# A linear-attention and feed-forward kernel: one small transposition goes from the tensor engine to a transposing transfer, and one denominator from matmuls to VectorE

## The chip, the core and the metric

The kernel runs on one core of a Trainium2 chip. The metric is the device time of one execution in microseconds (us); smaller is better. Before the change the median of three runs is 283.37 us (283.28 to 283.57).

## What is computed

Linear attention with phi(x) = elu(x) + 1 for 8 batches, 8 heads, 576 tokens and 64 channels a head, and then a feed-forward layer over all 4608 tokens. Inputs and output are float32; the kernel works in bfloat16 with float32 sums.

```
def phi(x):
    return np.where(x > 0, x, np.exp(x) - 1.0) + 1.0
q_p, k_p = (phi(q), phi(k))
kv = np.einsum('bhsd,bhse->bhde', k_p, v)
z = np.sum(k_p, axis=2)
num = np.einsum('bhsd,bhde->bhse', q_p, kv)
den = np.einsum('bhsd,bhd->bhs', q_p, z)[..., None] + 1e-06
attn = num / den
# x: attn as (4608 tokens, 512)
h = x @ w_in            # 512 -> 2048
g = h - np.tanh(h)
out = g @ w_out         # 2048 -> 512
```

## The kernel before, in words

**Chunks and slots.** The feed-forward layer runs in nine chunks of 512 tokens (loop over `c`). Chunks 0 to 7 hold the first 512 tokens of a batch each, chunk 8 the last 64 tokens of all eight batches (the "rest"). A chunk has two stages. Stage 1 has 16 slots `s1[0..15]`: in each, four matmuls of 128x512 (L458) make one block of `h`; after every second slot ScalarE takes the tanh of two blocks (L464) and VectorE subtracts, which writes `gT` (L465). Blocks go through PSUM banks 0 to 5 in turn, so block 6 needs bank 0 back, which the first subtraction of the chunk frees. Stage 2 has 16 slots `s2[0..15]` of four matmuls each (L479); four slots make one tile of 128 tokens, which ScalarE copies out (L490) and SyncE (SP) stores in two transfers (L503).

**Attention in the gaps.** The attention of a later batch is put into the slots by hand as lambdas. Each engine works in the order in which its instructions are written down; a scheduler changes nothing. In chunk `c`, with `n1 = c + 1` and `n2 = c + 2`, the batch `n2` gets its phi (`a_kphi`, `a_qphi`: exp on ScalarE L151, two operations on VectorE L152 and L153), its `kv` matmuls (L198, together with a column that sums `k`, which is `z`) inside `a_num`, and batch `n1` its numerator matmuls (`num_mm` L279, `rest_mm` L288).

**Two ways to divide.** Batches 0 to 2 (`b < QS`) make the denominator with matmuls (`a_den`, L371) and multiply the numerator by the reciprocal; for batch 2 the reciprocal goes out to DRAM and comes back spread over partitions (`a_spread`: `ds` L400, `rdb` L403, both on SP), and `num_scale` (L429) writes `xT`. Batches 3 to 7 divide q before the numerator: `kz_copy` copies `z` out of PSUM repeated 64 times (`zr`, L218); `q_zb` turns `zr` by two matmuls against an identity (L227) and ScalarE copies the result to `zb` (L230); GpSimd (POOL) multiplies phi(q) by `zb` in two halves (`q_prod`, L237); VectorE sums over the channels in four pieces (`q_den`, L242); `q_scale` takes the reciprocal (L248), GpSimd scales phi(q) (L251), and a transposing transfer issued by SP (`a_qT_dma`, L170) turns it for the numerator matmuls.

**Where these stand.** `a_num` is in `s2[12]` for `c == 1` and in `s2[9]` after that; `q_zb` and `q_prod` two slots later. For `c > 1` the first two `q_den` are in `s2[15]`, which puts them on VectorE ahead of the next chunk's first `gT`. The float32 loads of `k`, `q` and `v` are issued by GpSimd (L104): those of batch `n2 + 1` in `s2[9]` for `c` from 2 to 4, those of batch 3 in `s1[0]` and those of batch 4 in `s2[15]` of chunk 1. `k` and `q` have one buffer each, so a load waits for the last reader of the batch before.

**The rest tokens of batches 0 and 1.** `r_phi` (phi and a transposing transfer of `qTr`, L327) is in `s2[1]` of chunk 4; in `s2[9]` of chunk 6 `r_den` makes their denominator with eight matmuls (L335), takes the reciprocal (L338, L340) and spreads it through DRAM (L343, L347), `r_num` makes the numerators, and in `s1[3]` of chunk 7 `r_scale` multiplies (L359).

**Batch 2's k.** Its two exp are in `s1[1]` and `s1[3]` of chunk 1, its two `r` operations (L152) stand at the end of chunk 0, and its two minima (L153) in `s1[3]` and `s1[5]`. `a_den` and `a_spread` of batch 2 are in `s1[12]`.

Of the kernel before, what the change touches and what calls it, by code (L numbers as in the profile page):

```python
# [11 lines left out]
F32 = mybir.dt.float32  # L12
BF16 = mybir.dt.bfloat16
AF = mybir.ActivationFunctionType
ALU = mybir.AluOpType
# [3 lines left out]
def kernel(  # L19
# [9 lines left out]
    nc = tc.nc  # L29
    B, H, S, D = q.shape  # L30
# [58 lines left out]
    def rest_at(b):  # L89

        return 512 * B + 64 * b
# [120 lines left out]
    def kz_copy(b, b0, o):  # L212
        ps = ps_all[:, b0:b0 + 2, o:o + 132].rearrange("p g (i e) -> p g i e", i=2)
        if b < QS:
            nc.vector.tensor_mul(kz_t[b][:, :, :, 64:96], ps[:, :, :, 64:65].to_broadcast([128, 2, 2, 32]), mask)
        else:
            zr_t[b] = rpool.tile([128, 2, 2, 64], BF16, name="zr")
            nc.vector.tensor_copy(zr_t[b].rearrange("p i g t -> p g i t"),  # L218
                                  ps[:, :, :, 64:65].to_broadcast([128, 2, 2, 64]))
        nc.vector.tensor_copy(kz_t[b][:, :, :, 0:64], ps[:, :, :, 0:64])  # L220


    def q_zb(b, bank):

        ps = ps_all[:, bank, 0:256]
        for i in range(2):
            nc.tensor.matmul(ps[:, 128 * i:128 * i + 128], zr_t[b][:, i].rearrange("p g t -> p (g t)"), ident,  # L227
                             start=True, stop=True)
        zb_t[b] = rpool.tile([128, 2, 128], BF16, name="zb")
        nc.scalar.copy(zb_t[b].rearrange("p i x -> p (i x)"), ps)  # L230

    def q_prod(b):

# [48 lines left out]
    def rest_mm(b, b0, o, qT=None):  # L282

        kz, j = kz_t[b], J - 1 if qT is None else 0
        qT = qT_t[b] if qT is None else qT
        for i in range(2):
            for rs, cs, h, hg in quads():
                nc.tensor.matmul(ps_all[cs, b0 + h, 64 * i + o:64 * i + o + 64], kz[rs, hg, i, 0:64],  # L288
                                 qT[rs, i, j, hg, :], start=True, stop=True)
        return [ps_all[:, b0 + h, o:o + 128].rearrange("p (i t) -> p i t", i=2) for h in range(2)]  # L290
# [27 lines left out]
    def r_phi():  # L318

        x = qr.rearrange("p b i h d -> p (b i h d)")  # L320
        e, r = (epool.tile([128, 2, J, D], BF16, name=n).rearrange("p h j d -> p (h j d)")[:, 0:8 * D] for n in "er")
        y = const.tile([128, 8 * D], BF16, name="qpr")
        nc.scalar.activation(e, x, AF.Exp)
        nc.vector.tensor_scalar(r, x, 0.0, 1.0, ALU.max, ALU.add)
        nc.vector.tensor_tensor(y, e, r, ALU.min)
        qT_t["r"] = const.tile([128, 2, 2, 2, 64], BF16, name="qTr")
        nc.sync.dma_start_transpose(out=qT_t["r"].rearrange("p b i g t -> p (b i) (g t)"), in_=y)  # L327

    def r_den(bank, o):

        qT = qT_t["r"]
        ps = ps_all[0:64, bank, o:o + 64]
        for n, p in enumerate((0, 2, 1, 3)):
            for b in range(2):
                nc.tensor.matmul(ps[32 * b:32 * b + 32], kz_t[b][:, p // 2, p % 2, 64:96], qT[:, b, p % 2, p // 2, :],  # L335
                                 start=(n == 0), stop=(n == NP - 1))
        den = const.tile([64, 64], F32, name="denr")
        nc.vector.tensor_scalar(den, ps, 1e-6, None, ALU.add)  # L338
        rden = const.tile([64, 64], F32, name="rdenr")
        nc.vector.reciprocal(rden, den)  # L340
        ds = dram.tile([2, H, 64], F32, name="dsr")
        for b in range(2):
            nc.sync.dma_start(out=ds[b], in_=rden[32 * b:32 * b + H])  # L343
        rdb = rdb_t["r"] = const.tile([128, 2, NP, 64], F32, name="rdbr")
        for b in range(2):
            for hh in range(2):
                nc.sync.dma_start(  # L347
                    out=rdb[64 * hh:64 * hh + 64, b].rearrange("p a t -> p (a t)"),
                    in_=ds[b, 4 * hh:4 * hh + 4].rearrange("a t -> (a t)").partition_broadcast(64))

    def r_num(b0, o):

        pr_t["r"] = [rest_mm(b, b0, o + 128 * b, qT_t["r"][:, b].unsqueeze(2)) for b in range(2)]

    def r_scale():

        for b in range(2):
            for h, ps in enumerate(pr_t["r"][b]):
                nc.vector.tensor_mul(xT[:, 2 * h:2 * h + 2, rest_at(b):rest_at(b) + 64], ps,  # L359
                                     rdb_t["r"][:, b, 2 * h:2 * h + 2])  # L360

    def a_den(b, bank, parts=range(4)):

# [266 lines left out]
    for c in range(NC):  # L630
# [4 lines left out]
        if c == 0:  # L635
            sub = {}

            def spread1():
                a_spread_pe(1, range(NP))
                for p in range(NP):  # L640
                    a_scale(1, p, sub["ns"], p)

            def kv1():
                kv_cols_mm(1, 4, 0)
                kz_copy(1, 4, 0)

            def num1():
                ns = sub["ns"] = new_ns(1)
                for i in (1, 0):
                    b0 = 4 + 2 * i  # L650
                    num_mm(1, i, lambda h: b0 + h)
                    nc.scalar.copy(ns[:, i::2, 0:8, :].rearrange("p a j t -> p a (j t)"), ps_all[:, b0:b0 + 2, :])

            def vp1():
                a_vp1(0, nc.vector.tensor_copy)
                a_vp1(1, nc.scalar.copy)

            s1[13].append(lambda: a_qphi(1, 0))
            s1[14].append(lambda: a_qphi(1, 1))
            s2[0].append(lambda: a_kphi(1, 0))  # L660
            s2[2].append(lambda: ([f() for i in range(2) for f in a_qT_pe(1, i, Banks([4 + 2 * i, 5 + 2 * i]))], load_q(2)))
            s2[3].append(lambda: (a_kphi(1, 1), load_k(2)))
            s2[4].append(prepare)
            s2[6].append(lambda: a_vp(1, 0))
            s2[8].append(lambda: (vp1(), load_v(2)))
            s2[9].append(kv1)
            s2[10].append(lambda: (a_den(1, 4), num1(), a_split(1)))
            s2[13].append(spread1)

            qs, ks = [], []  # L670

            def exp2(pieces, src, store, name, i):
                pieces.append(phi_pieces(2, src, store, name, i))
                pieces[i][0]()

            def rest2(f):
                f[1]()
                f[2]()

            def k2(i):  # L680
                ks.append(phi_pieces(2, k_t, kp_t, "kp", i))
                ks[i][1]()

            s2[14].append(lambda: exp2(qs, q_t, qp_t, "qp", 0))
            s2[15].append(lambda: (exp2(qs, q_t, qp_t, "qp", 1), rest2(qs[0]), rest2(qs[1]), a_qT_dma(2), [f() for f in later], k2(0), k2(1)))
        elif n1 < B:
            if c == 1:
                def kv2():
                    kv_cols_mm(2, 6, 0)
                    kz_copy(2, 6, 0)  # L690

                s1[10].append(kv2)
            if n1 < QS:
                s1[12].append(lambda: (a_den(n1, 6), a_spread(n1)))
            else:
                if c == 2:
                    s1[2].append(lambda: (q_den(n1, 0, 0), q_den(n1, 0, 1)))
                e = 2 * (c == 2)
                s1[3 + e].append(lambda: q_den(n1, 1, 0))
                s1[5 + e].append(lambda: q_den(n1, 1, 1))  # L700
                s1[7 + e].append(lambda: q_scale(n1))
            m = 12 if c == 1 else 9
            if c == 3:
                s1[12].append(load_qr)
            if c == 4:
                s2[1].append(r_phi)
            if c == B - 2:
                s2[m].append(lambda: (r_den(7, 384), r_num(6, 128)))
            s2[m].append(lambda: a_num(n1, n2 if n2 < B else 0))
            if n2 < B:  # L710
                s2[m + 2].append(lambda: (q_zb(n2, 4 if c == 1 else 7), q_prod(n2)))
                if c > 1:
                    s2[15].append(lambda: (q_den(n2, 0, 0), q_den(n2, 0, 1)))
        if c == B - 1:
            s1[3].append(r_scale)
        if c == 1:
            for i in range(2):
                s1[1 + 2 * i].append(lambda i=i: ks[i][0]())
                s1[3 + 2 * i].append(lambda i=i: ks[i][2]())
            s1[0].append(lambda: (a_vp(2, 0, nc.gpsimd), a_vp(2, 1, nc.gpsimd),  # L720
                                  gate(qT_t[n1]), load_k(n2), load_q(n2), load_v(n2)))
        if c >= 1 and n2 < B:
# [100 lines left out]
```

## Time and profile before

| what | value |
|---|---|
| median of 3 runs | 283.37 us |
| time of the profiled execution | 283.29 us |
| span of its instructions | 281.5 us (1.79 us of the time lie outside) |
| granted TensorE clock | 1.00 |
| TensorE (PE) busy | 276.1 us (98%) |
| VectorE (DVE) busy | 176.9 us (63%) |
| ScalarE (ACT) busy | 146.0 us (52%) |
| GpSimd (POOL) busy | 81.9 us (29%) |

Busy time is the union of an engine's instructions. The profile also gives groups of instructions (count, busy time, mean duration), the idle time of an engine and what ended it, the chain of work that ended last, timelines of one engine, and for transfers the time from issue to landing (the last update of the semaphore). Queue q0 carries the loads issued by GpSimd, queue q1 the transfers issued by SP.

### The profile page before, as it was taken

How to read it: one execution, taken by the hardware profiler on the slowest of the kernel's cores; microseconds unless marked ns; L12 is line 12 of the kernel's file. 1: busy time of each engine (PE TensorE's matmuls, PEld its weight loads, DVE VectorE, ACT ScalarE, POOL GpSimd, SP SyncE). 2: the span in 40 equal slices, each digit the busy share in tenths (PEclk: the TensorE clock that was granted, in tenths of full speed). 3: DMA queues.
4: the chain of work that ended last, by engine and by line, in shares of the span. 5: the costliest groups of instructions: out<-in, count | busy, mean ns of one | idle time of the engine just before them, and what ended most of it. 6: DMA issues, size and time to landing. Idle time of an engine off the chain costs nothing.

```text
span 281.5 us, 5103 instructions
## 1 busy us (share of the span) xinstructions
PE 276.1 (98%) x2085; PEld 131.0 (47%) x2085; DVE 176.9 (63%) x285; ACT 146.0 (52%) x177; POOL 81.9 (29%) x79
## 2 busy tenths in 40 slices
PE   8899999999999999999999999999999999999995
PEld 3574544444544454445444544454444444444443
DVE  5759967993879755976398839763961177006600
ACT  4747918856255654675357636673541365126411
POOL 8642330320092434362623361406050000000000
PEclk9999999999999999999999999999999999999999
DMA  6999999799829899079904990342025210230023
GB/s 102 189 205 207 205 207 206 158 196 213 228 46 204 117 199 214 1 123 161 207 18 96 173 222 18 73 90 67 8 43 118 77 36 2 51 78 20 2 66 83
DMA packets 40135, 33.25 MB, mean 118 GB/s; under 512 B 17744, under 2 KB 35824, under 8 KB 39984
## 3 DMA queue, kind: packets, MB, share of 16 engines
q0 software_dynamic: 18688, 18.35, 41.5%
q1 hardware_dynamic: 21424, 14.58, 21.9%
q8 instruction: 16, 0.26, 0.3%
q14 instruction: 7, 0.06, 0.0%
HBM read 38.14 MB, written 9.46 MB: 169 GB/s over the span
## 4 chain that ended last, share of the span: by engine, by line
PE 91%; DMA 4%; DVE 1%; ACT 1%; issue 1%; POOL 1%; SPq 0%; DVEq 0%; POOLq 0%
PE ps_all L458 43%; PE ps_all L479 41%; DMA out_dram<-osb 3%; DMA kraw<-in_k_dram 2%; PE ps_all L198 2%; PE ps_all L742 1%; PE ps_all L279 1%; ACT osb L490 1%; SPq L503 0%; PE ps_all L309 0%; POOL qraw L101 0%; ACT e L151 0%; PE ps_all L182 0%; PE ps_all L371 0%; DVE rden L380 0%
## 5 line engine op out<-in xcount | busy, mean ns | idle before, releaser
L479 PE MATMUL ps_all<-w_out_sb,gT 128*128 128x512 bf16 x560 | 124.6, 379 | 0.0
L458 PE MATMUL ps_all<-xT,w_in_sb 128*128 128x512 bf16 x560 | 122.8, 379 | 0.0
L465 DVE TENSOR_TENSOR gT<-ps_all,th 128x1024 bf16<-128x1024 f32 x64 | 77.7, 1217 | 45.2 <-ACT th L464 45.2
L464 ACT ACTIVATE th<-ps_all 128x1024 f32<-128x1024 f32 x64 | 65.6, 1024 | 46.7 <-PE ps_all L458 46.7
L458 PEld LDWEIGHTS <-w_in_sb 128*128 128x128 bf16 x560 | 54.6, 98 | 65.7 <-issue 0.3
L479 PEld LDWEIGHTS <-gT 128*128 128x128 bf16 x560 | 53.8, 98 | 63.2 <-issue 0.2
L490 ACT COPY osb<-ps_all 128x512 f32<-128x512 f32 (+1 forms) x36 | 20.7, 582 | 56.9 <-PE ps_all L479 46.3
L237 POOL TENSOR_TENSOR pr<-qp,zb 128x1152 f32<-128x1152 bf16 x10 | 23.4, 2359 | 37.8 <-ACT zb L230 37.8
L251 POOL TENSOR_TENSOR qp<-qp,rd 128x1152 bf16<-128x1152 bf16 x10 | 21.0, 2115 | 36.9 <-issue 23.7
L242 DVE TENSOR_REDUCE dn<-pr 128x9 f32<-128x576 f32 x20 | 14.5, 746 | 12.2 <-POOL pr L237 12.2
L151 ACT ACTIVATE e<-qraw 128x1152 bf16<-128x1152 bf16 (+1 forms) x16 | 18.2, 1135 | 3.6 <-DMA qraw<-in_q_dram 3.6
L151 ACT ACTIVATE e<-kraw 128x1152 bf16<-128x1152 bf16 x15 | 17.5, 1165 | 0.0
L153 DVE TENSOR_TENSOR kp<-e,r 128x1152 bf16<-128x1152 bf16 x15 | 11.9, 792 | 4.1 <-ACT e L151 3.2
L153 DVE TENSOR_TENSOR qp<-e,r 128x1152 bf16<-128x1152 bf16 (+1 forms) x16 | 11.9, 742 | 4.0 <-ACT e L151 3.0
L568 PE MATMUL ps_all<-zero 128*128 128x512 bf16 x29 | 9.2, 475 | 1.2 <-DVE zero L513 1.2
L124 POOL DMA_DIRECT2D w_out_sb<-in_moe_w_out_dram x10 | 6.4, 637 | 10.1 <-DMA w_in_sb<-in_moe_w_in_dram 4.7
L104 POOL DMA_DIRECT2D kraw<-in_k_dram x7 | 5.5, 783 | 11.0 <-ACT e L151 10.6
L202 DVE COPY vp<-v 128x1152 bf16<-128x1152 bf16 x11 | 6.0, 542 | 4.0 <-DMA v<-in_v_dram 4.0
L470 DVE TENSOR_TENSOR gT<-ps_all,th 128x512 bf16<-128x512 f32 x12 | 7.9, 686 | 0.6
L104 POOL DMA_DIRECT2D qraw<-in_q_dram x7 | 5.3, 752 | 9.9 <-ACT e L151 5.2
L469 ACT ACTIVATE th<-ps_all 128x512 f32<-128x512 f32 x12 | 7.2, 596 | 1.9 <-DVE gT L748 1.0
L420 ACT CAST xT<-ps_all 128x1024 bf16<-128x1024 f32 x5 | 5.1, 1012 | 5.1 <-PE ps_all L288 4.4
(108 smaller groups left out, 146.8 us busy)
## 6 DMA issues: line engine op xcount, KB each, us to landing
out_dram<-osb SPq DMA_DIRECT2D x65, 128.0 KB, 2.4
kraw<-in_k_dram POOLq DMA_DIRECT2D x7, 576.0 KB, 7.0
qraw<-in_q_dram POOLq DMA_DIRECT2D x6, 576.0 KB, 8.7
v<-in_v_dram POOLq DMA_DIRECT2D x6, 576.0 KB, 12.4
w_in_sb<-in_moe_w_in_dram POOLq DMA_DIRECT2D x3, 512.0 KB, 9.8
v<-in_v_dram POOLq DMA_DIRECT2D x4, 288.0 KB, 8.7
rdb<-ds SPq DMA_DIRECT2D x2, 576.0 KB, 5.7
w_out_sb<-in_moe_w_out_dram POOLq DMA_DIRECT2D x4, 256.0 KB, 11.7
```

What stands on the lines that cost most here:

```text
L104: nc.gpsimd.dma_start(out=t[:, :, :, 0:n].rearrange("q h i j d -> q (h i) (j d)"), in_=x.rearrange("(n q) x -> q n x", n=4))
L151: return (lambda: nc.scalar.activation(e, x, AF.Exp), lambda: nc.vector.tensor_scalar(r, x, 0.0, 1.0, ALU.max, ALU.add), lambda: nc.vector ...
L153: lambda: nc.vector.tensor_tensor(y, e, r, ALU.min))
L237: nc.gpsimd.tensor_mul(pr_t[b][:, i].rearrange("p j h d -> p j (h d)"), qp_t[b][:, i].rearrange("p j h d -> p j (h d)"), zb_t[b][:, i].uns ...
L242: nc.vector.tensor_reduce(dn_t[b][:, i, :, h], pr_t[b][:, i, :, h, :], mybir.AxisListType.X, ALU.add)
L251: nc.gpsimd.tensor_mul(x, x, rd[:, i].unsqueeze(2).to_broadcast([128, J * 2, D]))
L458: nc.tensor.matmul(h, w_in_sb[:, p, fi * 128:(fi + 1) * 128], xT[:, p, c * 512:(c + 1) * 512], start=(n == 0), stop=(n == NP - 1))
L464: nc.scalar.activation(th, h, AF.Tanh)
L465: nc.vector.tensor_sub(gT[:, fi:fi + 2, :], h, th)
L479: nc.tensor.matmul(o, gT[:, fi, i * 128:(i + 1) * 128], w_out_sb[:, fi, :], start=(fi == 0), stop=(fi == NF - 1))
L490: nc.scalar.copy(osb[:, f0:f1], o[:, f0:f1])
L568: nc.tensor.matmul(ps_all[:, 0, :], zero[:, 0:128], zero, start=True, stop=True)
```

## The change

Three edits. First, `q_zb` is gone: for batches 3 to 7 `kz_copy` lets SP issue a transposing transfer `zb <- zr` (two blocks of 128x128) directly after the copy that makes `zr`. Second, the rest tokens of batches 0 and 1 are divided before their numerator: `r_z` (VectorE, `s2[13]` of chunk 3) takes their `z` from `kz`, repeats it, and a transposing transfer of four blocks makes `zbr`; `r_scale` (VectorE, `s2[12]` of chunk 4) multiplies, sums, takes the reciprocal and scales, and only then `qTr` is transposed; `r_den`, its DRAM trip and the multiplications of chunk 7 are gone, and `r_copy` copies the numerators out. Third, in chunk 1 the second `r` operation of batch 2's k moves from the end of chunk 0 to `s1[5]`, and `a_den` with `a_spread` of batch 2 from `s1[12]` to `s1[13]`. In the order of each engine nothing else moves, except that SP now has `zb` ahead of the stores of the fourth tile in chunk 1 and of the third tile in chunks 2 to 5, and `zbr` and `qTr` between stores of chunks 3 and 4.

```diff
@@ kz_copy
             zr_t[b] = rpool.tile([128, 2, 2, 64], BF16, name="zr")
             nc.vector.tensor_copy(zr_t[b].rearrange("p i g t -> p g i t"),
                                   ps[:, :, :, 64:65].to_broadcast([128, 2, 2, 64]))
+            zb_t[b] = rpool.tile([128, 2, 128], BF16, name="zb")
+            nc.sync.dma_start_transpose(out=zb_t[b], in_=zr_t[b].rearrange("p i g t -> p (i g t)"))
         nc.vector.tensor_copy(kz_t[b][:, :, :, 0:64], ps[:, :, :, 0:64])
-    def q_zb(b, bank):
-        ps = ps_all[:, bank, 0:256]
-        for i in range(2):
-            nc.tensor.matmul(ps[:, 128 * i:128 * i + 128], zr_t[b][:, i].rearrange("p g t -> p (g t)"), ident,
-                             start=True, stop=True)
-        zb_t[b] = rpool.tile([128, 2, 128], BF16, name="zb")
-        nc.scalar.copy(zb_t[b].rearrange("p i x -> p (i x)"), ps)
@@ r_phi, r_z, r_scale, r_num, r_copy
         nc.vector.tensor_tensor(y, e, r, ALU.min)
+        qp_t["r"] = y
+    def r_z():
+        zs = const.tile([128, 2, 2, 2], BF16, name="zsr")
+        zr = const.tile([128, 2, 2, 2, 64], BF16, name="zrr")
+        for b in range(2):
+            nc.vector.tensor_reduce(zs[:, b], kz_t[b][:, :, :, 64:72], mybir.AxisListType.X, ALU.max)
+            nc.vector.tensor_copy(zr[:, b].rearrange("p i g t -> p g i t"),
+                                  zs[:, b].unsqueeze(3).to_broadcast([128, 2, 2, 64]))
+        zb_t["r"] = const.tile([128, 4, 128], BF16, name="zbr")
+        nc.sync.dma_start_transpose(out=zb_t["r"], in_=zr.rearrange("p b i g t -> p (b i g t)"))
+    def r_scale():
+        y = qp_t["r"]
+        pr = const.tile([128, 8, D], F32, name="prr")
+        nc.vector.tensor_mul(pr.rearrange("p n d -> p (n d)"), y, zb_t["r"].rearrange("p n x -> p (n x)"))
+        dn = const.tile([128, 8], F32, name="dnr")
+        nc.vector.tensor_reduce(dn, pr, mybir.AxisListType.X, ALU.add)
+        nc.vector.tensor_scalar(dn, dn, 1e-6, None, ALU.add)
+        rd = const.tile([128, 8], F32, name="rdr")
+        nc.vector.reciprocal(rd, dn)
+        x = y.rearrange("p (n d) -> p n d", d=D)
+        nc.vector.tensor_mul(x, x, rd.unsqueeze(2).to_broadcast([128, 8, D]))
         qT_t["r"] = const.tile([128, 2, 2, 2, 64], BF16, name="qTr")
         nc.sync.dma_start_transpose(out=qT_t["r"].rearrange("p b i g t -> p (b i) (g t)"), in_=y)
-    def r_den(bank, o):
...
+    def r_copy(b0, o):
+        for h, copy in enumerate((nc.vector.tensor_copy, nc.scalar.copy)):
+            copy(xT[:, 2 * h:2 * h + 2, rest_at(0):rest_at(2)].rearrange("p i (b t) -> p b i t", b=2),
+                 ps_all[:, b0 + h, o:o + 256].rearrange("p (b i t) -> p b i t", b=2, i=2))
@@ the slots
             def k2(i):
                 ks.append(phi_pieces(2, k_t, kp_t, "kp", i))
-                ks[i][1]()
+                if not i:
+                    ks[i][1]()
...
-                s1[12].append(lambda: (a_den(n1, 6), a_spread(n1)))
+                s1[13].append(lambda: (a_den(n1, 6), a_spread(n1)))
...
             if c == 3:
                 s1[12].append(load_qr)
+                s2[13].append(r_z)
             if c == 4:
                 s2[1].append(r_phi)
-            if c == B - 2:
-                s2[m].append(lambda: (r_den(7, 384), r_num(6, 128)))
-            s2[m].append(lambda: a_num(n1, n2 if n2 < B else 0))
+                s2[12].append(r_scale)
+            s2[m].append(lambda: (c == B - 2 and r_num(6, 128), a_num(n1, n2 if n2 < B else 0),
+                                  c == B - 2 and r_copy(6, 128)))
             if n2 < B:
-                s2[m + 2].append(lambda: (q_zb(n2, 4 if c == 1 else 7), q_prod(n2)))
+                s2[m + 2].append(lambda: q_prod(n2))
...
-        if c == B - 1:
-            s1[3].append(r_scale)
...
-                s1[3 + 2 * i].append(lambda i=i: ks[i][2]())
+                s1[3 + 2 * i].append(lambda i=i: (i and ks[i][1](), ks[i][2]()))
```

More of the change, by code (lines that the diff above doesn't have):

```diff
@@ L326, in r_phi @@
         qT_t["r"] = const.tile([128, 2, 2, 2, 64], BF16, name="qTr")
         nc.sync.dma_start_transpose(out=qT_t["r"].rearrange("p b i g t -> p (b i) (g t)"), in_=y)
-    def r_den(bank, o):
[L331 to L341, printed above, removed]
-        for b in range(2):
[L343 to L360, printed above, removed]
+    def r_num(b0, o):
+        for b in range(2):
+            rest_mm(b, b0, o + 128 * b, qT_t["r"][:, b].unsqueeze(2))
```

## The prediction

> **What bounds the kernel now.** I read the page first: who is busy, and which engine makes the chain.
>
> ```profile
> PE 276.1 (98%) x2085; PEld 131.0 (47%) x2085; DVE 176.9 (63%) x285; ACT 146.0 (52%) x177; POOL 81.9 (29%) x79
> PE 91%; DMA 4%; DVE 1%; ACT 1%; issue 1%; POOL 1%; SPq 0%; DVEq 0%; POOLq 0%
> ```
>
> PE is busy for 98% of the span at a granted clock of 1.00, and its matmuls run back to back (64 of 128x512 in 13.81 us, 0.2158 us each). So every matmul taken off PE is time off the end, and every wait put before one is added to it. Next the chain of waits, at the places that the change touches: the start of chunk 1, one stage 2, and the numerators of chunk 6.
>
> ```profile
> 47.29 9.64 PE ps_all L458 x44
> ...
> 103.34 0.11 PE ps_all L227 x2
> 103.45 3.45 PE ps_all L479 x16
> 106.90 13.81 PE ps_all L458 x64
> ...
> 216.75 0.24 PE ps_all L335 x8
> 216.99 0.02 issue
> 217.01 0.23 DVE denr L338
> 217.24 0.04 issue
> 217.28 0.32 PE ps_all L288 x15
> 217.60 0.43 PE ps_all L279 x8
> ```
>
> The two turning matmuls cost 0.11 us a batch, the eight denominator matmuls with what follows 0.85 us, and the 44 matmuls of chunk 1 take 0.14 us more than 44 x 0.2158 = 9.50. Third, since `zb` has its readers on GpSimd and VectorE, their timeline around one of these places (chunk 2 into 3):
>
> ```profile
> 101.57 0.42 DVE L218 CAST zr<-ps_all 128x256 bf16<-128x256 f32 x1 [0.58 <-PE ps_all L198]
> 104.32 4.68 POOL L237 TENSOR_TENSOR pr<-qp,zb 128x1152 f32<-128x1152 bf16 x2 [2.34 <-ACT zb L230]
> 106.71 1.42 DVE L242 TENSOR_REDUCE dn<-pr 128x9 f32<-128x576 f32 x2 [3.05 <-POOL pr L237]
> 109.72 1.23 DVE L465 TENSOR_TENSOR gT<-ps_all,th 128x1024 bf16<-128x1024 f32 x1 [1.60 <-ACT th L464]
> ```
>
> VectorE waits 3.05 us for the first half of `pr`, and the chunk's first `gT` is queued behind that. Last, how long SP's transfers take there: the view of the stores from 97 to 109 us, its columns least, median and most, then the queues from 162.3 to 165.9 us.
>
> ```profile
> DMA to landing us min/median/max: 5.7/6.0/6.3
> q0 software_dynamic: 601, 0.67, 117.1%
> ```
>
> Queue q1 has no line in the second answer: in these 3.6 us it moved not one packet, though a store issued at 162.30 was waiting. The same holds from 105.5 to 107.4 and from 134.3 to 136.9. In chunk 5, where nothing is loaded, the stores take 2.2/2.3/2.4.
>
> **Part by part.** *What PE loses.* Five `q_zb`: 5 x 0.11 = 0.55. In chunk 6 the stretch from 216.75 to the numerators at 217.60 (0.85) shrinks to the sixteen L288 matmuls, 2 x 0.06 by the rows of eight in other chunks, plus 0.13 for the first small matmul after the large ones (L279 takes 0.56 there and 0.43 here): 0.25. Saved 0.60. Together 1.15 us. PE has nothing to fill in, so all of it counts.
>
> *Batch 2's k.* VectorE runs both `r` from 50.44 to 51.26, and the first `gT` of chunk 1 starts at 51.18, though its tanh was done at 50.24; it ends at 52.40, and block 6 starts at 52.45 where 47.12 + 24 x 0.2158 = 52.30 was due. That is the 0.14. With one `r` (0.41) less the `gT` ends near 52.0 and the wait goes. The moved `r` (0.45) makes the `kz` copy of batch 2 later (about 59.8 for 59.3), and `a_den`, one slot (0.86) later, just clears it. Late next is the last `gT` of the chunk: add and reciprocal (0.30 + 1.05) now stand ahead of it, so it ends near 65.0, against a first use near 65.2. I take 0.14 saved, with 0 to 0.14 as bounds.
>
> *Batch 2's reciprocal.* It is ready near 63.8 for 62.2. Its way is `ds`, then `rdb` on SP, then L429. In before `rdb` lands at 75.84 and L429 starts at 75.94; its fourth piece is ready 2.48 later at 78.42, and PE wants it at 77.63 + 5 x 0.216 = 78.71. Of this cover of 0.29, PE's own 0.25 lead (0.14 + 0.11) eats nearly all, so a later `rdb` is a stall of the same length. How much later? The `ds` transfers took 4.1 us from issue to landing, where the same kind (`dsr`) took 1.2 in chunk 6: they lay behind stores that landed until 65.57. If the stores set it, `rdb` moves by 0; if the 4.1 repeats, by 1.6. In the same stretch the load of batch 3's k waits for the moved `r`: 56.3 for 55.9. I take 0.3, nearer to the stores.
>
> *The way of z.* Before: `zr` ends at 101.99, the matmuls, a copy on ScalarE (0.38), and `zb` is there at 104.24. After: SP issues the transfer at 102.04 (it is free: the stores before it were issued by 100.28). No row shows a transfer of two transposed blocks. `qTr` (four blocks) landed 2.44 after issue with nothing loading, `qT` (eighteen) 4.65; the line through them gives 2.1 for two. In between loads the nearest rows are the stores, 128 KB to 64.
>
> How late may it be? `pr` starts 0.08 after `zb` and its half takes 2.36; two L242 and the `gT` behind them take 2.54, and with two hand-overs (0.08) `gT` ends 5.06 after `zb`. Block 6 of chunk 3 is due at 106.74 + 5.18 = 111.92, and 0.11 earlier without L227: `zb` must land by 106.75, which is 4.7 after its issue. The same sum gives 4.7 for chunks 3 and 4 (issues at 131.25 and 160.35).
>
> Chunk 1 (4.7 does not apply, the sums are in slots 2 and 5 and have 2 us to spare) and chunk 5 (no loads, 2.1) cost nothing. In chunks 2, 3 and 4 GpSimd's loads run: stores took 6.0, 5.5 and 6.1 (the medians; least 5.7, 4.7 and 6.1, most 6.3, 6.5 and 6.1). Less 0.2 for the smaller transfer (2.1 against 2.3) and less 4.7, PE stalls 1.1 + 0.6 + 1.2 = 2.9. The bounds: with the least, 0.8 + 0 + 1.2 = 2.0; with the most, 1.4 + 1.6 + 1.2 = 4.2; and with 2.1, none at all. I take 2.9, since every store that was issued while a load ran took at least 3.9, and `zb`, issued 0.7 to 1.5 us after the load of q, is inside.
>
> [...]
>
> *The rest tokens.* `r_z` on VectorE: two reductions (0.16, L617) and two copies (0.23 to 0.43): 0.8 to 1.2, in chunk 3 after the `xT` copies, inside the 3.05 in which VectorE waits for `pr`. `r_scale` in chunk 4: two products of 512 (0.43 by L325 to 0.68 by L429), a sum of 512 (0.74 by L242), 0.17 and 0.38: 2.2 to 2.7, in the same 3.05, which a late `zb` only widens. If it overran by all of 2.7, the first `gT` would take 1.6 of it in idle time and PE 0.9, so at most 0.2 would show. Their two transfers stand on SP ahead of stores, whose buffers are five tiles (17 us) deep; `qTr` is needed 50 us later. `r_copy` adds 0.38 to ScalarE before a copy that waited 0.68 for PE, and 0.43 to VectorE in a 6.76 gap. Nothing for all of these; ScalarE's five copies of 0.38 go, also for nothing.
>
> **Sum** against the profiled execution of 283.29: - 1.15 - 0.14 + 0.3 + 2.9 = + 1.9, 285.2; the median stood 0.08 above it, so 285.3.
>
> **Rivals.** *Faster: the transfer is in time.* If `zb` lands within 4.7 us of its issue in all three chunks (its packets slip through at the seam between the loads of k and q, as q1's did from 131.0 to 132.5, 226 packets of it), PE keeps the 1.29: 282.1, or 282.4 with the 0.3 of `rdb`. For it: the queue had finished its stores just before each of the three spots. Against it: the medians above. It decides at 4.7. *Worse: it misses the seam everywhere* and lands with the store issued after it (110.04, 140.11 and 168.09): 3.3, 4.2 and 3.0 later than allowed at the very most, 10.5 in sum; with the store's own time from issue in its place (6.05, 6.91, 5.78) it is 1.35 + 2.2 + 1.1 = 4.65, and with `rdb` late by 1.3 the total is 283.37 - 1.29 + 4.65 + 1.3 = 288.0. *No change:* one chunk alone stalls (1.2), with 0.1 for `rdb`: 283.4. That the change does not do what it says can be left out: PE's order has the ten and the eight matmuls gone.
>
> **How the numbers follow.** Some stall in two or three chunks, 0.68 (forecast 285.3; of this 0.1 above 288.0); one chunk alone, 0.07; in time everywhere, 0.25. A difference of 0.2% (0.57 us) is about what a measurement of this kernel can tell from none, so these are the chances of slower, same and faster. The range holds the faster case whole and the late one to 288.0: 282.1 to 288.0, with about 0.1 above it and a little below. The slower case alone would run from 284.1 (stalls of 2.0, no `rdb`) to 288.0.
>
> **What would show it.** Right: `zb` lands 5 to 6.5 after its issue in chunks 2 to 4 and 2.1 in chunk 5; VectorE waits 5 and not 3.05 us for `pr`; PE has waits on `gT` at block 6 of chunks 3, 4 and 5, of about 1 us each, and none in chunk 6. L227 and L335 are gone, and the 44 matmuls of chunk 1 take 9.50. Wrong: `zb` lands within 4.7, or VectorE puts its first `gT` elsewhere; then PE has no new wait and the time is near 282.

## The result and the profile after

| | before | after |
|---|---|---|
| median, us (lowest to highest) | 283.54 (283.28 to 284.01) | 296.29 (293.88 to 298.11) |
| profiled execution, us (its span) | 283.29 (281.5) | 295.85 (294.1) |
| PE busy, us | 276.1 | 278.8 |

The changed kernel is slower: the ratio is 1.0437, with a 95% interval from 1.0383 to 1.0491. The prediction said slower, but 285.3 us with a range to 288.0, so the size was far off. Line numbers below are those of each kernel; in the changed one L227, L335 and their followers are gone, stage 1's matmuls are L453, `gT` L460, `pr` L229, the sums L234 and the numerators' scaling L424.

The page after, two lines: who is busy, and the granted clock in 40 slices.

```profile
PE 278.8 (95%) x2067; PEld 130.8 (44%) x2067; DVE 178.6 (61%) x289; ACT 144.8 (49%) x173; POOL 82.0 (28%) x79
PEclk9999999999999999899999998899999999999999
```

PE has 18 matmuls fewer and is busy 2.7 us longer, and three slices have an 8: twice PE ran at a lower clock. The prediction's sum has no term for that. Next, what PE waited for (us in total, times, longest):

```profile
PE ps_all L453 <- DVE gT L460: 7.8, 3, 3.1
PE ps_all L453 <- DVE xT L424: 1.4, 3, 1.1
```

The first line is the predicted wait, three times over, at 2.6 us each in place of 1; the second is the late `rdb` of batch 2. The timelines around the start of chunk 3 (start, duration, what, idle time before and its releaser), from 103 us of GpSimd and of VectorE, and from 112 of PE:

```profile
111.32 4.68 POOL L229 TENSOR_TENSOR pr<-qp,zb 128x1152 f32<-128x1152 bf16 x2 [7.38 <-DMA zb<-zr]
```

```profile
113.71 1.41 DVE L234 TENSOR_REDUCE dn<-pr 128x9 f32<-128x576 f32 x2 [8.10 <-POOL pr L229]
115.04 2.35 DVE L460 TENSOR_TENSOR gT<-ps_all,th 128x1024 bf16<-128x1024 f32 x2
```

```profile
111.83 2.10 PE L453 MATMUL ps_all<-xT,w_in_sb 128*128 128x512 bf16 x9
116.31 5.95 PE L453 MATMUL ps_all<-xT,w_in_sb 128*128 128x512 bf16 x19 [2.38 <-DVE gT L460]
```

GpSimd waits for `zb`, VectorE for `pr` (8.10 us, where it was 3.05), the first `gT` stands behind the sums, and PE stands behind that `gT`. The nineteen matmuls from there on take 5.95 us where 18 x 0.2158 + 0.38 = 4.26 was due: seven of them are spaced 0.43 us. Last, the transfers of `zb` from issue to landing in us (least, median, most). The view has only the two whose semaphore updates are all recorded, those of chunks 3 and 4; by the last update of each, chunks 2, 3 and 4 are 7.26, 7.21 and 7.94, and chunk 5, without loads, is 2.72:

```profile
DMA to landing us min/median/max: 7.2/7.6/7.9
```

**The account.** Stalls, as the end of the waiting matmul less that of the one before and less 0.216: 2.54 + 2.49 + 3.31 = 8.34 for `gT`, 1.93 for `rdb`. Two stretches of half clock: 1.7 + 1.6. Saved: 1.15 + 0.14. That makes + 12.3, and the profiled execution is 12.6 longer; the other 0.3 lies in the start-up, since chunk 1 begins at 47.41 and in the kernel before at 47.12. The six times differ by how many such stretches they have, by the mean clock: 293.88 and 294.16 at 0.994, 295.85 to 296.99 at 0.988, 298.11 at 0.983, some 1.7 us for each.

### The profile page after: what moved, and what is told of

Same layout as the page of the kernel before. It is cut to its first block, busy times and chain, and to the rows that moved or that the text cites. A ratio compares the mean times of both kernels' runs of the same rounds, so it can differ in the third digit from the quotient of the medians.

```text
span 294.1 us, 5065 instructions
## 1 busy us (share of the span) xinstructions
PE 278.8 (95%) x2067; PEld 130.8 (44%) x2067; DVE 178.6 (61%) x289; ACT 144.8 (49%) x173; POOL 82.0 (28%) x79
## 5 line engine op out<-in xcount | busy, mean ns | idle before, releaser
L453 PE MATMUL ps_all<-xT,w_in_sb 128*128 128x512 bf16 x560 | 126.9, 386 | 9.2 <-DVE gT L460 7.8
L460 DVE TENSOR_TENSOR gT<-ps_all,th 128x1024 bf16<-128x1024 f32 x64 | 77.5, 1218 | 40.3 <-ACT th L459 40.1
L453 PEld LDWEIGHTS <-w_in_sb 128*128 128x128 bf16 x560 | 55.4, 99 | 78.3 <-issue 15.5
L229 POOL TENSOR_TENSOR pr<-qp,zb 128x1152 f32<-128x1152 bf16 x10 | 23.4, 2358 | 56.7 <-DMA zb<-zr 56.7
L234 DVE TENSOR_REDUCE dn<-pr 128x9 f32<-128x576 f32 x20 | 14.5, 746 | 25.2 <-POOL pr L229 25.2
L415 DVE CAST xT<-ps_all 128x1024 bf16<-128x1024 f32 x5 | 6.1, 1217 | 7.0 <-PE ps_all L280 7.0
L563 PE MATMUL ps_all<-zero 128*128 128x512 bf16 x29 | 8.5, 445 | 1.2 <-DVE zero L508 1.2
## 6 DMA issues: line engine op xcount, KB each, us to landing
w_in_sb<-in_moe_w_in_dram POOLq DMA_DIRECT2D x3, 512.0 KB, 10.5
v<-in_v_dram POOLq DMA_DIRECT2D x4, 288.0 KB, 8.9
```

What stands on the lines that cost most here:

```text
L229: nc.gpsimd.tensor_mul(pr_t[b][:, i].rearrange("p j h d -> p j (h d)"), qp_t[b][:, i].rearrange("p j h d -> p j (h d)"), zb_t[b][:, i].uns ...
L234: nc.vector.tensor_reduce(dn_t[b][:, i, :, h], pr_t[b][:, i, :, h, :], mybir.AxisListType.X, ALU.add)
L453: nc.tensor.matmul(h, w_in_sb[:, p, fi * 128:(fi + 1) * 128], xT[:, p, c * 512:(c + 1) * 512], start=(n == 0), stop=(n == NP - 1))
L460: nc.vector.tensor_sub(gT[:, fi:fi + 2, :], h, th)
L563: nc.tensor.matmul(ps_all[:, 0, :], zero[:, 0:128], zero, start=True, stop=True)
```

## The experiments

Of each run the time stands beside that of the kernel before on the same chip (283.7 to 283.8).

**One edit at a time: `z_only`.** The kernel before with the first edit alone.

```
...
+            nc.sync.dma_start_transpose(out=zb_t[b], in_=zr_t[b].rearrange("p i g t -> p (i g t)"))
...
-                s2[m + 2].append(lambda: (q_zb(n2, 4 if c == 1 else 7), q_prod(n2)))
+                s2[m + 2].append(lambda: q_prod(n2))
```

> Only the first edit on the kernel before: zb by the transposing transfer, nothing else. Theory A (the late zb makes the loss): PE loses 5 x 0.11 = 0.55 us of matmuls, zb lands 7 to 8 us after its issue in chunks 2, 3 and 4, and block 6 of the next chunk waits for what goes beyond 4.7 us: 2.5 + 2.5 + 3.3 = 8.3 us, with one to three stretches of half clock behind these waits at 1.7 us each. Time 293 to 296.5 us. Theory B (VectorE's rest-token work and SP's two extra transfers, or batch 2's late rdb, make the loss): without them little is left, at most the 2.9 us of the prediction, 282.8 to 285.7 us. Where the granted clock shows no stretch below full, the time under theory A is 291.

Measured 293.29 us (291.44 to 294.49), ratio 1.0318 (1.0281 to 1.0355). PE's waits in its profile:

```profile
PE ps_all L460 <- DVE gT L467: 7.3, 3, 3.0
```

Theory A holds. This execution took 292.67: 283.72 - 0.55 + stalls of 2.20 + 3.14 + 2.45 + one stretch of half clock at 1.7 = 292.7. The fastest run, 291.44, has a mean clock of 0.999 and so no such stretch; the stalls alone make 283.72 - 0.55 + 7.8 = 291.0.

**`rest_only`.** The kernel before with the second edit alone (`r_z`, `r_scale`, `r_copy` for `r_den` and its DRAM trip, as in the diff above).

> Only the second edit on the kernel before: the rest tokens' denominators on VectorE. Theory A: PE loses 0.60 us at the numerators of chunk 6, and nothing is late: 282.8 us. Theory B (the VectorE work of chunks 3 and 4 pushes the first gT of the next chunk, or zbr and qTr on SP push stores): 0.2 to 3 us of waits of PE on gT at the starts of chunks 4 and 5: 283.5 to 286 us.

Measured 283.71 us, ratio 0.9993 (0.9978 to 1.0008): no difference, where theory A wanted 0.9 us. The 0.60 is there: from the numerators of chunk 5 to the stage-2 matmul behind those of chunk 6 PE takes 29.83 us, before 30.43. But the profile has two new stalls, 0.29 at the start of chunk 2 (`rdb`, whose `ds` took 4.0 to 4.8 us in this execution) and 0.15 at block 6 of chunk 5, so 0.16 is left of it. The second one comes from VectorE and GpSimd, whose timelines around it are:

```profile
164.47 1.70 DVE L345 TENSOR_SCALAR dnr<-dnr 128x8 f32<-128x8 f32 x1
166.21 0.20 DVE L347 RECIPROCAL rdr<-dnr 128x8 f32<-128x8 f32 x1
166.44 2.58 DVE L349 TENSOR_TENSOR qpr<-qpr,rdr 128x512 bf16<-128x512 bf16 x1
```

```profile
163.78 4.70 POOL L236 TENSOR_TENSOR pr<-qp,zb 128x1152 f32<-128x1152 bf16 x2 [2.34 <-DVE prr L342]
```

An addition to eight numbers takes 1.70 us and ends at 166.17, when GpSimd's first product (2.35 of the 4.70, from 163.78) has just ended at 166.13; the multiplication then lasts until 169.02, past the end of the second at 168.48. In the changed kernel, where `pr` starts later, the same two take 0.17 and 0.69. VectorE's sum just before (L344, from 163.75 to 164.44) ran beside the same GpSimd product and kept its 0.69. The reciprocal between the two ran beside the second product and took 0.20, in the changed kernel 0.20 as well. So the addition and the multiplication are long beside a GpSimd product and the sum and the reciprocal are not; why these two, no run shows.

**`k2_only`.** The kernel before with the third edit alone.

```
-                ks[i][1]()
+                if not i:
+                    ks[i][1]()
...
-                s1[12].append(lambda: (a_den(n1, 6), a_spread(n1)))
+                s1[13].append(lambda: (a_den(n1, 6), a_spread(n1)))
...
-                s1[3 + 2 * i].append(lambda i=i: ks[i][2]())
+                s1[3 + 2 * i].append(lambda i=i: (i and ks[i][1](), ks[i][2]()))
```

> Only the third edit on the kernel before: the second r operation of batch 2's k in slot 5 of chunk 1, a_den and a_spread one slot later. Theory A (the account of the changed kernel): the wait of 0.14 us at block 6 of chunk 1 goes, rdb lands about 2 us later than the 75.84 of before, and PE loses what exceeds the cover of 0.29, less 0.14 + 0.11 that is no longer there to be eaten: 1.6 us at the start of chunk 2. Time 284.9 us. Theory B (the prediction: rdb hardly later): 283.3 us.

Measured 285.50 us, ratio 1.0051 (1.0033 to 1.0069). Its waits of PE:

```profile
PE ps_all L458 <- DVE xT L429: 0.8, 3, 0.4
PE ps_all L279 <- DMA qT<-qp: 0.7, 1, 0.7
```

The size is nearer to theory A's 284.9, the make-up only in part. `rdb` lands at 77.58 for 75.84 (0.40 of this is a later start-up) and costs 0.53 + 0.38 + 0.33 = 1.24 us of stalls (the view counts less, since it leaves the small hand-overs out); another 0.78 is PE waiting for batch 3's `qT` in chunk 2, which was issued 1.5 us later than before, beside a load of k, and took 7.05 us for 5.39. The changed kernel doesn't have this second wait: there the same transfer took 5.08.

**`k2_r_alone`.** The same with `a_den` and `a_spread` left in slot 12.

> The kernel before with the first half of the third edit: the second r operation of batch 2's k in slot 5 of chunk 1, while a_den and a_spread stay in slot 12. Theory A (the slot later of a_den is what made rdb late by 1.7): PE waits 0.4 to 0.5 us on kz at a_den, the reciprocal is ready about 0.4 later than before, rdb lands 0.4 to 0.8 later, PE stalls 0.1 to 0.5 at the start of chunk 2: 283.7 - 0.14 + 0.5 to 1.0 = 284.1 to 284.6 us. Theory H (the moved r alone, through the later load of batch 3's k and what follows on the queues, makes rdb late): rdb lands 1.7 later and the time is 285.3 us or more.

Measured 284.10 us, ratio 1.0001 (0.9980 to 1.0022). Theory H is out: `rdb` did not stall PE at all, and the moved slot is what made it late: counted from the start of chunk 1 it lands after 28.72 us in the kernel before, 29.22 here and 30.06 in `k2_only`. Theory A is right on that, on PE's 0.4 at `a_den` and on the size to within the interval, and wrong on the stall: the one after `a_den`, 0.71, is on `qT` here too. What the third edit's r operation gives by itself can't be told from nothing.

**Are the loads the cause? `loads_late`.** The changed kernel, with one number changed.

```
-                s2[15 if c == 1 else 9].append(lambda: (load_k(n2 + 1), load_q(n2 + 1), load_v(n2 + 1)))
+                s2[15 if c == 1 else 12].append(lambda: (load_k(n2 + 1), load_q(n2 + 1), load_v(n2 + 1)))
```

> The changed kernel, with GpSimd's loads of k, q and v of the batch after next three slots later in chunks 2, 3 and 4, so that GpSimd issues them after its product pr and no load runs while zb is under way. Theory A (the loads make zb late): zb lands 2.1 to 2.8 us after its issue, as in chunk 5; no wait of PE on gT at block 6 of chunks 3 to 5, no stretch of half clock; what stays is the late rdb of batch 2 at 1.9 us: 283.3 - 1.3 + 1.9 = 284 us. Theory C (a transposing transfer of this shape is slow beside anything on SP's queue, stores included): zb stays above 6 us and the time near 296.

Measured 284.52 us, ratio 1.0024 (1.0001 to 1.0046), some 12 us less than the changed kernel for three slots. The landing of `zb` in chunks 1 to 4 of its profile, beside the line above:

```profile
DMA to landing us min/median/max: 2.3/3.0/5.0
```

Theory A holds in its main point and C falls (the 5.0 is in chunk 1, behind `rdb`; chunk 2 took 3.44, more than theory A's 2.8, but less than 4.7). What the transfer does beside a load is seen in the queues of the changed kernel in chunk 4, where `zb` was issued at 168.78, first from 170.40 to 172.00 us, then from 173.60 to 175.20 (packets, MB, share of 16 engines):

```profile
q0 software_dynamic: 251, 0.29, 111.9%
```

```profile
q0 software_dynamic: 174, 0.20, 93.4%
q1 hardware_dynamic: 169, 0.04, 31.7%
```

The landing after 7.94 us has three parts. To 170.40 queue q1 still moves the stores that stood before `zb` (they landed at 170.35 and 170.65). Then, to 172.40, the load of q has everything: 319 packets, and none of q1. From there to 176.00 the two queues share, with about as many packets of the one as of the other in the middle; `zb` has 256 packets of 256 bytes. It lands at 176.72, and the load of q at 176.93. In `loads_late`, alone, they all move from 134.0 to 134.8 us (with some semaphore updates):

```profile
q1 hardware_dynamic: 287, 0.07, 39.8%
```

There is one stall left besides `rdb`'s 1.86: 0.69 at block 6 of chunk 5. Theory A had none. There `r_scale` runs beside `pr` again and takes 6.4 us (2.14 for the addition, 2.57 for the multiplication). Taking the late `zb` away uncovers it.

**`loads_late_alone`.** The kernel before with the same number changed.

> The kernel before, with the loads of chunks 2 to 4 three slots later and nothing else changed: the control for the runs with late loads. Theory A: loads were not late before and are not now; 283.7 us, no difference. Theory F (late loads gain or lose something of their own, by the stores, qT or the phi of the next batch): a difference of over 0.6 us either way, with a wait of PE at the numerators or of ScalarE on k.

Measured 283.75 us, ratio 0.9999 (0.9988 to 1.0009): theory A. The later loads gain nothing by themselves.

**Is it the queue behind the sums? `den_later`.** The changed kernel, `zb` as late as ever, the sums of chunks 3 to 6 moved, and `q_scale` there from slot 7 to 9.

```
...
-                    s2[15].append(lambda: (q_den(n2, 0, 0), q_den(n2, 0, 1)))
...
+                    s1[6].append(lambda: (q_den(n1, 0, 0), q_den(n1, 0, 1)))
+                    s1[8].append(lambda: q_den(n1, 1, 0))
+                    s1[9].append(lambda: q_den(n1, 1, 1))
```

> The changed kernel, with VectorE's sums over pr moved: for chunks 3 to 5 the first pair from the end of the chunk before into slot 6, behind the subtraction of blocks 4 and 5, the third to slot 8, the fourth and q_scale to slot 9. The transfers are not touched. Theory A (the late zb costs because the first gT is queued behind the sums that wait for it): zb lands 7 to 8 us after its issue as before, but PE has no wait on gT at block 6, no stretch of half clock follows, and what stays is the late rdb at 1.9 us: 284 to 284.5 us; q is divided about 2 us later, so the transfer of qT could become late for the numerators by up to 1 us a chunk, which would make it 287. Theory C (PE's stalls come from something else that the late loads also moved, the transfers' use of memory for one): the time stays near 293 to 296.

Measured 286.56 us, ratio 1.0108 (1.0085 to 1.0131), full clock in all runs. `zb` takes 6.96, 8.16 and 6.81 us in chunks 2 to 4, and PE's waits are

```profile
PE ps_all L474 <- DVE gT L460: 1.4, 4, 0.3
PE ps_all L453 <- DVE xT L424: 1.2, 3, 0.8
...
PE ps_all L271 <- DMA qT<-qp: 0.2, 1, 0.2
```

No stall at block 6 is left, so theory A holds in its main point: the transfer was late for VectorE's order, not for the work. The new price is at the start of stage 2, where the last `gT` now comes 0.505 late in each of four chunks, because the sums stand later among the subtractions. From the profiled execution of before, 283.29 - 1.29 + 1.71 (`rdb`) + 2.02 + 0.24 = 285.97, and the one of `den_later` took 285.86.

**The clock by itself: `clock_large` and `clock_small`.** The kernel before, no transfer touched, VectorE made late by repeating a sum (8 times, or 5).

```
-                    s2[15].append(lambda: (q_den(n2, 0, 0), q_den(n2, 0, 1)))
+                    s2[15].append(lambda: [q_den(n2, 0, h) for h in (0, 1)] + [q_den(n2, 0, 1) for _ in range(8 if c < 5 else 0)])
```

> The kernel before, with the second of the two sums in front of the first gT repeated eight times more (into the same tile) at the end of chunks 2, 3 and 4: 8 x 0.70 = 5.6 us more on VectorE, of which 1.6 us of its idle time and 0.97 us of PE's lead are cover, so PE stalls 3 x 3.0 = 9.1 us on gT with every transfer in time. Theory A (the clock falls where a window of 3.41 us, that runs on by itself, holds too few matmuls): one to three stretches of half clock of 3.41 us behind the stalls in most runs, 1.7 us each; 283.7 + 9.1 + 0 to 5.1 = 293 to 298 us, and the profiled run's drops lie where the window of 3.41 us that ended there held under 1.2 us of matmuls. Theory D (the clock falls because of the transfers, not of the stalls): full clock, 292.8 us in every run.

> The kernel before with the second of the two sums in front of the first gT repeated five times more at the end of chunks 2, 3 and 4 (eight times in clock_large, where PE stalled 3.53 us a chunk): three repeats less at 0.70, so stalls of 3 x 1.43 = 4.3 us. Theory A (half clock comes only where a window of 3.41 us holds less than some 1.0 to 1.4 us of matmuls; a stall of 1.4 leaves at least 2.0 in any window): no stretch of half clock in any run, 283.7 + 4.3 = 288.0 us. Theory G (any wait of PE can bring half clock, the longer the likelier): one or two stretches in some runs, 289.7 to 291.4 us there.

`clock_large` took 300.29 us (299.45 to 301.30), ratio 1.0588 (1.0560 to 1.0615); `clock_small` 287.46 (287.34 to 289.15), ratio 1.0142 (1.0117 to 1.0167). PE's waits on `gT`, in the first and in the second:

```profile
PE ps_all L458 <- DVE gT L465: 10.6, 3, 3.5
```

```profile
PE ps_all L458 <- DVE gT L465: 4.4, 4, 1.2
```

With stalls of 3.5 us each, the half clock came in every run, three times in the profiled one: 283.7 + 10.6 + 3 x 1.7 = 299.4, and it took 299.45. So theory D falls, and the expected 293 to 298 was too low, the stalls being 0.5 longer than worked out. With three stalls of 1.33 us it came in none of four runs (the view's fourth wait is the one at block 6 of chunk 1, 0.14 us in before and 1.09 in this execution), and 283.8 + 4.0 = 287.8: theory A, not G.

Where it came is read from windows of 3.41 us. In the changed kernel the clock fell at 117.08 and 181.93 us, for 3.413 us each. The full clock between them lasted 61.44, which is 18 times 3.413; before the first it lasted 112.64 and after the second 109.23, 33 and 32 times. So in this run the clock changed only on a raster of 3.413 us, wherever the stalls lay. These are the windows that ended at the two drops, the half-clock stretch after the first, and the two around the stall in chunk 4, after which nothing fell (length, PE busy and matmuls, granted clock, share of the DMA engines, GB/s):

```profile
113.67:117.08 3.41, 1.03 (x6) 1.00 0.26 68
117.08:120.49 3.41, 3.41 (x10) 0.50 0.00 0
144.39:147.80 3.41, 2.85 (x14) 1.00 1.31 187
147.80:151.21 3.41, 1.64 (x8) 1.00 0.40 68
178.52:181.93 3.41, 0.36 (x2) 1.00 0.60 82
```

The stalls of 2.54 and 2.49 us are equal, but the first lay in one window and left 1.03 us of matmuls in it, the second lay across two. In `z_only` the clock fell after the window with 1.13, and not after those with 1.53 and 1.72, though the last belongs to a stall of 3.14 (here the busy times of PEld, that is PE's weight loads, of VectorE, ScalarE and GpSimd stand between PE's and the clock):

```profile
110.60:114.02 3.42, 1.53 (x8) 0.59 (x6) 2.44 (x3) 0.87 (x1) 3.26 (x2) 1.00 0.59 141
144.74:148.15 3.41, 1.72 (x8) 0.78 (x8) 3.41 (x5) 1.02 (x1) 1.39 (x1) 1.00 0.06 16
175.45:178.87 3.42, 1.13 (x6) 0.48 (x5) 3.42 (x4) 0.95 (x1) 2.12 (x1) 1.00 0.00 1
```

In `clock_large` it fell after windows with 0.19, 0.14 and 0.34. So in these runs the bound lies between 1.13 and 1.53 us of matmuls in 3.41. Idle gaps of PE of 2.29 and 2.38 us (the stalls of 2.45 and 2.54) were enough.

One thing stays open. One of the ten runs of `loads_late` (287.24 us) and one of the twelve of `rest_only` (288.52) show a mean clock of 0.994, which is one such stretch, though after the start-up the longest stall in the profiles kept of these kernels is 1.15 and 0.29 us. No trace of these two runs was kept, so what stalled PE in them is not known.

**Both gains without the losses: `best_try`.** Edits one and two without the third, the loads three slots later, and `r_scale` in the first slot of stage 2 of chunk 6, where GpSimd does nothing.

```
...
-                s2[12].append(r_scale)
+            if c == B - 2:
+                s2[0].append(r_scale)
```

> Edits one and two of the change without the third, with the loads of chunks 2 to 4 three slots later, behind GpSimd's pr, and r_scale moved from chunk 4's slot 12, where it ran beside GpSimd's pr, to the first slot of stage 2 of chunk 6. Theory A: zb lands within 4.7 us of its issue, VectorE's scaling runs at its own speed, PE loses 0.55 + 0.60 us and waits for nothing new: 283.7 - 1.15 = 282.6 us. Theory E (the sums' gain is eaten by qTr, which lands only about 5 us after the start of that stage 2 and could hold the numerators): up to 1 us of it comes back as a wait of PE on qTr, 283.5 us.

Measured 282.52 us (282.03 to 283.34), ratio 0.9965 (0.9954 to 0.9977): faster than the kernel before, by 1.2 us. `zb` lands 2.3 to 3.6 after its issue, PE has no wait on `gT`, `xT` or `qTr` after the start-up, and VectorE's two operations have their own duration again:

```profile
211.45 0.17 DVE L338 TENSOR_SCALAR dnr<-dnr 128x8 f32<-128x8 f32 x1
211.66 0.20 DVE L340 RECIPROCAL rdr<-dnr 128x8 f32<-128x8 f32 x1
211.89 0.69 DVE L342 TENSOR_TENSOR qpr<-qpr,rdr 128x512 bf16<-128x512 bf16 x1
```

Theory A, to 0.1 us; `qTr` lands at 215.01, some 1.3 us before its matmuls, so E did not happen.

## Why the prediction was wrong, step by step

**Right.** *What PE loses*: 1.15 us, which `best_try` gives back whole. *How late `zb` may be*: latencies less 4.7 are 2.56, 2.51 and 3.24, the stalls 2.54, 2.49 and 3.31, at the matmul that was named. Chunks 1 and 5 cost nothing. The wait of 0.14 in chunk 1 went.

**Mis-sized: how long `zb` takes** (2.9 us of stalls taken, 4.2 at most; 8.34 measured). This is the step that failed. It took a store's time from issue to landing as if it belonged to the transfer. In these runs it went with the place in the load: in chunk 4, 1.6 us went by with the stores ahead, 2.0 with the load alone, and 3.6 with both queues at once. In chunks 2, 3 and 4 of the changed kernel `zb` landed 0.72, 0.28 and 0.21 us before the load of q. In `z_only`, where the first stall had not yet moved anything, `zb` was issued at 102.18, 1.8 us before the place of the store that the 6.0 came from, and landed at 109.11, 0.9 before that store's 110.04: sooner issued, it took longer, 6.93 us for 6.05. The prediction had this in hand as the rival's "very most", `zb` landing with the next store, 10.5 us in sum, but then priced that rival at 4.65 by the same latencies. The word for the faster rival, that the queue had finished its stores just before each spot, was wrong for all three: with `zb` due for issue at 102.04, 131.25 and 160.35, the stores before it landed until 106.03, 134.17 and 162.46. The stores' times were thin as well. Their views have only the transfers whose semaphore updates are all recorded, two stores of eight, three of eleven and one of six. By the last update of each the most was 7.14, 7.02 and 6.07 us, which by the same sum makes 2.2 + 2.1 + 1.2 = 5.5 us of stalls, still short of 8.34. And the least of 3.9 for a store issued while a load ran holds beside the loads of k, q and v alone: two stores of before, issued at 124.82 and 125.33 while the last 32 KB load of `qr` was out until 126.83, took 2.30 and 2.38.

**Missing: the clock.** Nothing in the profile before shows a clock below full, and the sum had no term for it: 3.3 us in the profiled execution, some 1.7 to 5 over the runs. At the predicted stalls of about 1 us it would not have come, as `clock_small` shows; it is a second price that, by an estimate from these runs, starts only with stalls over some 1.9 to 2.3 us (3.41 less 1.53, less 1.13), and only if they lie in one window.

**Mis-sized: batch 2's reciprocal** (0.3 taken between 0 and 1.6; 1.93). The upper bound was the nearer one: the `ds` transfers took 4.1 again. They were issued 1.9 us later, while the stores ahead of them landed at much the same time (65.41 for 65.57), so the stores did not set it. The loads beside them may have, which no run shows. The last `rdb` transfer then took 8.09 for 7.80. `k2_r_alone` shows that the slot of `a_den` decides.

**Right by luck: the rest tokens at nothing.** The cover named for `r_scale`, VectorE's 3.05 us of waiting for `pr`, is the time in which GpSimd works, and two of its five operations took 1.70 and 2.58 us there in `rest_only`, for 0.17 and 0.69 in the changed kernel. In the changed kernel the late `zb` moved `pr` away; with `zb` in time the cost is 0.15 to 0.69.

Where rivals stood: "misses the seam everywhere" is what happened, under a price that was too low, and the range ended at that price.

## What to carry to other kernels

Here a latency read off a queue beside a bulk load on the other queue did not carry over to a transfer put 1.8 us earlier: 6.05 us became 6.93, while the landings lay 0.9 apart. So for a transfer that is put earlier, take the time at which the next one in the queue landed, and keep the end of the load beside it, here 0.2 to 0.7 us after the transfer's, as a check. Before a matmul is replaced by a transfer, look what stands in order behind its reader, and whether the loads can go behind it; here three slots were worth 12 us. When a forecast has stalls of 2 us and more on TensorE, add the price of a slower clock: of the six of 2.20 to 3.31 us in the changed kernel and `z_only`, three brought 3.41 us at half clock, some 1.7 us each. When it hides VectorE's work in a wait, see that GpSimd is not what it waits for: in `rest_only` 0.69 us became 2.58.

## What the runs showed of the hardware

- In the changed kernel, `z_only` and `clock_large` the TensorE clock fell to half after six windows of 3.41 us with 0.14 to 1.13 us of matmuls, and not after three with 1.53, 1.64 and 1.72; in the changed kernel each fall lasted 3.413 us and cost 1.6 to 1.7.
- A transposing transfer of 256 packets took 2.3 to 3.6 us from issue to landing without loads on the other queue (4.6 to 5.0 behind a late `rdb`) and 6.8 to 8.2 beside them; in one of these its queue moved no packet for 2.0 us, and then its packets took 3.6 us beside the load's for 0.8 alone.
- An addition of 8 numbers a partition on VectorE took 1.70 and 2.14 us beside a GpSimd product, and 0.17 without one.
